# A decode block's tail: wo in one transfer, a layer norm with accumulated sums, and reader-less matmuls moved ahead of wo

## The chip, the cores and the metric

The kernel runs on one core of a Trainium2 chip. The metric is the device time of one execution in microseconds. The kernel before takes 186.57 us (median of 3 runs, 186.53 to 186.63).

## What is computed

One decode step of a block with modulated layer norms, attention over a cache, and a gated FFN, for two tokens (batch 2, one position) of width 640:

```python
mod = (silu(c) @ w_mod).reshape(2, 6, 1, 640)          # sa, ca, ga, sb, cb, gb
h = layernorm(x) * (1 + ca) + sa
q = (h @ wq) as 32 heads of 192
k, v = the last 1024 of 4096 cached positions, 32 heads of 192
o = softmax(q k^T / sqrt(192)) v
x = x + ga * (o @ wo)                                   # wo: 6144 x 640
h = layernorm(x) * (1 + cb) + sb
out = x + gb * ((gelu(h @ w_gate) * (h @ w_up)) @ w_down)   # F = 1536
```

The layer norm has no weights of its own and an epsilon of 1e-5. All inputs are bf16. With two tokens each weight and each cache element is used for next to nothing but two rows: 77 MB are read from HBM.

## The kernel before

**Order and queues.** The kernel is an order written by hand. Each engine has a list of operations (`S.op`, `S.dma`), and the helper derives the semaphore waits from the names of what an operation reads and writes. Each engine works off its list in order. All loads of weights and cache go out from SP's queue, in the order w_mod, wq, four loads of K, four of V, wo, w_gate, w_up, w_down. The few rows of `c` and `x` and the result go through ACT's queue.

**Places.** Three places of 128 partitions x 49,152 bytes hold K and V in turn (two halves of `pp`, and the start of `r1`). wq and later wo (61,440 bytes a partition) lie in `r1`; w_mod and later the three FFN weights lie in `pp`. A load is issued when the last reader of its place is done: wo after the last PV matmul of the first token (`keep["pv", 0, NTL - 1]`), the FFN weights after the second of four PV groups of the second token (`dead`, L595).

**wo.** Partition p holds rows 48p to 48p+47 of wo. `WO_SPLIT = [32, 16]` (L160) cuts them into two transfers, of 40,960 and 20,480 bytes per partition, each with a semaphore and a group of matmuls of its own (L607 to L615): for each row index t four matmuls of 160 columns, one in each quarter of the array, 128 in the first group and 64 in the second, all into one bank. `w_down` is cut likewise, into 8, 3 and 1 of 12 (L162).

**The layer norm** (L350 to L376) is used twice. Its values lie with a token's 640 columns in four groups of partitions, 160 columns each, two tokens side by side. DVE squares `X2[:, 0]` into `X2[:, 1]`, reduces both to two sums per partition (`st2`), a small f32 matmul with `Bsel` adds them over the partitions of a token (L355), and DVE and ACT make mean, variance, root and reciprocal as 128x1 columns. Three DVE instructions over 160 columns follow (`xn`, `mulc`, `out`), and a DVE transpose makes `hT`, the weights of the next matmuls.

**Matmuls without a reader.** `warm(n, bk)` (L455) issues n bf16 matmuls of 384 columns on `ident_b` and `qbc` into a bank that nobody reads. The K phase has four ahead of each reduction; in the tail three stand between gate and up (L634) and five after up (L638).

**The tail**, in TensorE's order: the PV matmuls of the second token, `sel` (four matmuls, L558, which bring the attention result into the layout of wo's weights, `oT`), wo, the statistics of the second layer norm, gate, three `warm`, up, five `warm`, and down in three groups (L648). DVE has `ga_attn` and `x1` (L617, L619) between wo and the layer norm, `geglu` (L639) and a transpose before down, and `gb_y` and `outC` at the end. ACT has the gelu (L635), which writes `gl`, a part of `Sg`, where the scores were.

Of the kernel before, what the change touches and what calls it, by code (L numbers as in the profile page):

```python
# [103 lines left out]
def bass_adaLN_cond__sliding_block_cached__geglu_ffn__decode_kernel(  # L104
# [15 lines left out]
    P = 128  # L120
# [19 lines left out]
    NPR = KP // PJ  # L140
    JH = J // 2
    NH = PJ // JH
# [9 lines left out]
    EPS = 1e-5  # L152
# [4 lines left out]

    NP = 3
    SL = PJ * Dh
    WO_SPLIT = [32, 16]  # L160
    assert sum(WO_SPLIT) == NT and NT * QP == Dh
    WD_SPLIT = [8, 3, 1]  # L162
    assert sum(WD_SPLIT) == FT
# [8 lines left out]
    with es:  # L172
        S = _Sched(nc, es)
        sb = lambda name, shape, dt: es.enter_context(nc.sbuf_tensor(name, shape, dt))
# [22 lines left out]
        ident_f = sb("ident_f", [P, P], F32)  # L197
# [3 lines left out]
        Bsel = sb("Bsel", [P, P], F32)  # L201
# [8 lines left out]
        X2 = sb("X2", [P, 2, DN], F32)  # L210
        st2 = sb("st2", [P, 2], F32)
        mv = sb("mv", [P, 4], F32)
        rstd = sb("rstd", [P, 1], F32)
        modC = sb("modC", [P, 6, DN], F32)
        opc = sb("opc", [P, 2, DN], F32)
        lnt = sb("lnt", [P, 2, DN], F32)
        hC = sb("hC", [P, DN], BF16)
        hT = sb("hT", [P, KT, SQ], BF16)

        Sg = sb("Sg", [P, max(2 * KP, FN)], F32)  # L220
        S_sb = Sg[:, 0:2 * KP].rearrange("p (b r) -> p b r", b=2)
        gl = Sg[:, 0:FN]
# [10 lines left out]
        ps = es.enter_context(nc.psum_tensor("ps", [P, 8, 512], F32))  # L233

        BK_T = 2
# [9 lines left out]
        def bank(k):  # L245
            return ("bank", k)
# [14 lines left out]
        def k_dma(dst, src):  # L261
            return lambda e: e.dma_start(dst, src)  # L262


        def rows_of(tile):
            return tile[0:P:BS, :]

        def dram_rows(v):
            return v.rearrange("b (j n) -> j b n", j=NJ)
# [2 lines left out]
        S.op("pool", lambda e: e.memset(xc[:, :], 0.0), writes=["xc"], name="xc0")  # L272
        S.op("pool", lambda e: e.memset(cx[:, :, :], 0.0), writes=["cxa", "cxb"], name="cx0")
        S.op("pool", lambda e: e.memset(scx[:, :, :], 0.0), writes=["scx"], name="scx0")
        S.dma("act", k_dma(rows_of(cc), dram_rows(c[:, :])), sem_c, writes=["cc"], name="ld_c")
        S.dma("act", k_dma(rows_of(xc), dram_rows(A_x[:, 0, :])), sem_x, writes=["xc"], name="ld_x")
        S.dma("act", k_dma(cx[:, :, 0:XS * KT], c[:, 0:XP * XS * KT].rearrange("b (i n) -> i b n", i=XP)), sem_cx, writes=["cxa"], name="ld_cxa")
# [5 lines left out]
             reads=["Sk"], writes=["ident_f"], name="ident_f")  # L283
        S.op("pool", lambda e: e.tensor_copy(out=ident_b[:, :], in_=ident_f[:, :]),
             reads=["ident_f"], writes=["ident_b"], name="ident_b")
# [33 lines left out]
        for o in range(4):  # L319
# [5 lines left out]
              sem_wq, writes=place_keys(2) + ["wq"], name="ld_wq")  # L325
# [21 lines left out]
        to_contraction(scT[:, :, :], sc[:, :], KT, ["sc"], ["scT"], "scT")  # L347
        S.op("dve", lambda e: e.tensor_copy(out=X2[:, 0, :], in_=xc[:, :]), reads=["xc"], writes=[("X2", 0)], name="x_f32")

        def layer_norm(tag, opc_idx, s_idx):  # L350
            S.op("dve", lambda e: e.tensor_tensor(out=X2[:, 1, :], in0=X2[:, 0, :], in1=X2[:, 0, :], op=ALU.mult),
                 reads=[("X2", 0)], writes=[("X2", 1)], name=tag + "_sq")
            S.op("dve", lambda e: e.tensor_reduce(out=st2[:, :], in_=X2[:, :, :], axis=AX.X, op=ALU.add),
                 reads=[("X2", 0), ("X2", 1)], writes=["st2"], name=tag + "_sum")
            S.op("pe", lambda e: e.matmul(ps[:, BK_T, SC:SC + 2], lhsT=Bsel[:, :], rhs=st2[:, :], start=True, stop=True),  # L355
                 reads=["st2", "Bsel"], writes=[bank(BK_T)], name=tag + "_stat")
            S.op("dve", lambda e: e.tensor_scalar(out=mv[:, 0:2], in0=ps[:, BK_T, SC:SC + 2], scalar1=1.0 / D, scalar2=None, op0=ALU.mult),
                 reads=[bank(BK_T)], writes=[("mv", 0)], name=tag + "_mean")
            S.op("dve", lambda e: e.scalar_tensor_tensor(out=mv[:, 2:3], in0=mv[:, 0:1], scalar=-1.0, in1=mv[:, 0:1],
                                                         op0=ALU.mult, op1=ALU.mult),  # L360
                 reads=[("mv", 0)], writes=[("mv", 1)], name=tag + "_nmsq")
            S.op("dve", lambda e: e.scalar_tensor_tensor(out=mv[:, 2:3], in0=mv[:, 1:2], scalar=EPS, in1=mv[:, 2:3],
                                                         op0=ALU.add, op1=ALU.add),
                 reads=[("mv", 0), ("mv", 1)], writes=[("mv", 1)], name=tag + "_var")
            S.op("act", lambda e: e.activation(out=mv[:, 3:4], in_=mv[:, 2:3], func=ACTF.Sqrt),
                 reads=[("mv", 1)], writes=[("mv", 2)], name=tag + "_sqrt")
            S.op("dve", lambda e: e.reciprocal(out=rstd[:, :], in_=mv[:, 3:4]),
                 reads=[("mv", 2)], writes=["rstd"], name=tag + "_rstd")
            S.op("dve", lambda e: e.tensor_scalar(out=lnt[:, 0, :], in0=X2[:, 0, :], scalar1=mv[:, 0:1], scalar2=rstd[:, 0:1],
                                                  op0=ALU.subtract, op1=ALU.mult),  # L370
                 reads=[("X2", 0), ("mv", 0), "rstd"], writes=[("lnt", 0)], name=tag + "_xn")
            S.op("dve", lambda e: e.tensor_tensor(out=lnt[:, 1, :], in0=lnt[:, 0, :], in1=opc[:, opc_idx, :], op=ALU.mult),
                 reads=[("lnt", 0), ("opc", opc_idx)], writes=[("lnt", 1)], name=tag + "_mulc")
            S.op("dve", lambda e: e.tensor_tensor(out=hC[:, :], in0=lnt[:, 1, :], in1=modC[:, s_idx, :], op=ALU.add),
                 reads=[("lnt", 1), ("modC", s_idx // 3)], writes=["hC"], name=tag + "_out")
            to_contraction(hT[:, :, :], hC[:, :], KT, ["hC"], ["hT"], tag + "_T")  # L376

        MB = (7, 4)
# [76 lines left out]
        def warm(n, bk):  # L455
            def f(e):
                last = None
                for i in range(n):
                    put = e.matmul if i == 0 else lambda *a, **k: held(e, *a, **k)
                    last = put(ps[:, bk, 0:2 * Dh], lhsT=ident_b[:, :], rhs=qbc[:, :, :].rearrange("p b d -> p (b d)"),  # L460
                               start=True, stop=True)
                return last
            S.op("pe", f, reads=["ident_b", "qbc"], writes=[bank(bk)], name="warm")
# [122 lines left out]
        assert state["next"] == len(items)  # L586
        p_sel()

        wo_src = A_wo.rearrange("(p t) n -> p t n", t=NT)
        wo_of = [(sum(WO_SPLIT[:i]), sum(WO_SPLIT[:i + 1])) for i in range(len(WO_SPLIT))]  # L590
        for i, (ta, tb) in enumerate(wo_of):
# [5 lines left out]
              writes=["wg"], deps=dead, name="ld_wg")  # L597
        S.dma("sp", k_dma(wu_v.rearrange("p k n -> p (k n)"), B_w_up.rearrange("(p k) n -> p (k n)", k=KT)), sem_wu,
              writes=["wu"], deps=dead, name="ld_wu")
# [7 lines left out]
        for i, (ta, tb) in enumerate(wo_of):  # L607
            def f(e, ta=ta, tb=tb):
# [7 lines left out]

        S.op("dve", lambda e: e.tensor_tensor(out=lnt[:, 0, :], in0=ps[:, BK_M, 0:DN], in1=modC[:, 2, :], op=ALU.mult),  # L617
             reads=[bank(BK_M), ("modC", 0)], writes=[("lnt", 0)], name="ga_attn")
        S.op("dve", lambda e: e.tensor_tensor(out=X2[:, 0, :], in0=lnt[:, 0, :], in1=X2[:, 0, :], op=ALU.add),  # L619
             reads=[("lnt", 0)], writes=[("X2", 0)], name="x1")  # L620
        layer_norm("ln2", 1, 3)

        def ffn_gu(bk, wv, key, name, ka, kb):
# [7 lines left out]
            S.op("pe", f, reads=["hT", key], writes=[bank(bk)], name="ffn_" + name)  # L631

        ffn_gu(BK_G[0], wg_v, "wg", "wg", 0, KT)
        warm(3, MB[0])  # L634
        S.op("act", lambda e: e.activation(out=gl, in_=ps[:, BK_G[0], 0:FN], func=ACTF.Gelu_apprx_tanh),  # L635
             reads=[bank(BK_G[0])], writes=["gl"], name="gelu")
        ffn_gu(BK_G[1], wu_v, "wu", "wu", 0, KT)
# [56 lines left out]
```

## Time and profile before

| | |
|---|---|
| median of 3 runs | 186.57 us |
| profiled execution, time | 186.42 us |
| profiled execution, span | 185.1 us |
| read from HBM | 76.88 MB, 415 GB/s over the span |
| queue of SP | 2596 packets, 76.87 MB, 96.8% of 16 engines' span |
| TensorE (matmul) busy | 110.3 us, 60% |
| VectorE (DVE) busy | 101.4 us, 55% |
| ScalarE (ACT) busy | 14.7 us, 8% |
| chain that ended last | DMA 56%, DVE 31%, PE 8% |

The span runs from the first to the last instruction; the time of an execution is a little more. Times inside the profile count from the span's start. PE is TensorE, PEld its weight loads, DVE VectorE, ACT ScalarE, POOL GpSimd, and SP the engine that issues the loads. A bracket behind an instruction says how long the engine had sat idle before it, and what ended the wait. The chain is followed back from the last instruction, at each step to what released it.

### The profile page before, as it was taken

Reading aid. Unit: us, or ns where it says so; the run is one execution under the profiler, and the core shown is the slowest. Engines: PE = TensorE matmul, PEld = TensorE weight load, DVE = VectorE, ACT = ScalarE, POOL = GpSimd, SP = SyncE. Lnnn points to the kernel's source line nnn. Section 1 sums busy time; section 2 is a strip of 40 time slices with the busy share of each in tenths; the row PEclk is TensorE's granted clock in tenths of the full one; section 3 lists DMA queues with packets and bytes.
Section 4 is the critical chain, followed back from the end, with each engine's and each line's share of the span. In section 5 each row is a group of like instructions: output and inputs, shape, how many; then the busy total and the mean of one; then the engine's idle time right before and its main releaser. Section 6 shows DMA issues by size and latency. Waiting matters only on the chain.

```text
span 185.1 us, 1892 instructions
## 1 busy us (share of the span) xinstructions
PE 110.3 (60%) x951; PEld 36.7 (20%) x721; DVE 101.4 (55%) x106; ACT 14.7 (8%) x24; POOL 5.3 (3%) x14
## 2 busy tenths in 40 slices
PE   0004900672079999988999885499468059093372
PEld 0001500340000000000000000266256036082211
DVE  5822400010588999999999994747565400302431
ACT  1103410023000000000000000200100000400310
POOL 8300000000000000000000000000000000000000
PEclk9999999998559999999999999569978858858579
DMA  7999999899999989899999989899999999899991
GB/s 261 392 486 469 451 425 417 372 471 404 446 435 414 490 350 510 382 467 396 446 446 404 488 361 499 372 488 396 446 425 425 453 434 425 376 417 427 420 389 58
DMA packets 2699, 76.99 MB, mean 416 GB/s; under 512 B 388, under 2 KB 644, under 8 KB 772
## 3 DMA queue, kind: packets, MB, share of 16 engines
q1 hardware_dynamic: 2596, 76.87, 96.8%
q8 instruction: 6, 0.10, 0.2%
q10 hardware_dynamic: 96, 0.01, 0.0%
q14 instruction: 1, 0.01, 0.0%
HBM read 76.88 MB, written 0.00 MB: 415 GB/s over the span
## 4 chain that ended last, share of the span: by engine, by line
DMA 56%; DVE 31%; PE 8%; SPq 3%; issue 1%; DVEq 0%
DMA pp<-in_A_k_cache_dram 23%; DMA pp<-in_B_w_down_dram 20%; DVE pp L467 19%; DMA pp<-in_A_v_cache_dram 12%; DVE r L467 7%; DVE Sg L487 5%; PE ps L533 4%; PE ps L453 3%; SPq L262 3%; PE ps L480 1%; PE ps L648 0%; DVE lnt L654 0%; DVE sc L656 0%; DVEq L93 0%; SPq L93 0%
## 5 line engine op out<-in xcount | busy, mean ns | idle before, releaser
L467 DVE TENSOR_TENSOR pp<-pp,qbc 128x6144 bf16<-128x6144 bf16 x12 | 40.1, 3348 | 8.5 <-DMA pp<-in_A_k_cache_dram 8.5
L453 PE MATMUL ps<-pp,ident_b 128*128 128x512 bf16 x132 | 31.7, 391 | 0.0
L533 PE MATMUL ps<-pp,Em 128*64 128x384 bf16 x192 | 21.5, 397 | 12.8 <-DMA pp<-in_A_v_cache_dram 11.6
L518 DVE TENSOR_TENSOR Em<-E_sb,M32b 128x2048 bf16<-128x2048 bf16 x8 | 18.2, 2288 | 7.2 <-PE ps L533 6.5
L533 PEld LDWEIGHTS ps<-pp,Em 128*64 128x64 bf16 x192 | 14.5, 134 | 19.5 <-issue 7.8
L467 DVE TENSOR_TENSOR r<-r,qbc 128x6144 bf16<-128x6144 bf16 x4 | 13.4, 3345 | 0.0
L389 PE MATMUL ps<-pp,scT 128*32 128x480 bf16 (+1 forms) x40 | 4.4, 595 | 14.7 <-DMA pp<-in_w_mod_dram 14.7
L487 DVE TENSOR_REDUCE Sg<-ps 128x32 f32<-128x512 f32 x16 | 10.9, 682 | 3.3 <-PE ps L453 3.3
L480 PE MATMUL ps<-pp,ident_b 128*128 128x512 bf16 x12 | 4.9, 407 | 12.7 <-DVE pp L467 12.7
L453 PE MATMUL ps<-qbc,ident_b 128*128 128x384 bf16 x54 | 12.1, 333 | 0.0
L423 PE MATMUL ps<-r,hT 128*32 128x512 bf16 x60 | 5.3, 532 | 10.6 <-DMA r<-in_A_wq_dram 10.6
L453 PE MATMUL ps<-r,ident_b 128*128 128x512 bf16 x44 | 10.1, 379 | 0.0
L550 DVE TENSOR_SCALAR On<-ps,rden 32x192 bf16<-32x192 f32 x4 | 1.7, 418 | 15.1 <-PE ps L533 15.1
L460 PEld LDWEIGHTS ps<-qbc,ident_b 128*128 128x128 bf16 x18 | 1.8, 98 | 37.8 <-issue 37.8
L434 DVE CAST qC<-ps 128x512 bf16<-128x512 f32 x1 | 0.7, 691 | 15.1 <-PE ps L423 15.1
L612 PE MATMUL ps<-r,oT 128*32 128x160 bf16 x192 | 5.8, 303 | 5.2 <-DMA r<-in_A_wo_dram 5.2
L507 ACT ACTIVATE E_sb<-Sg,nb 128x256 bf16<-128x256 f32 x2 | 1.0, 500 | 72.4 <-DVE nb L505 72.4
L460 PE MATMUL ps<-qbc,ident_b 128*128 128x384 bf16 x18 | 6.0, 336 | 0.7 <-ACT qbc L432 0.7
L612 PEld LDWEIGHTS ps<-r,oT 128*32 128x32 bf16 x192 | 5.3, 129 | 5.7 <-DMA r<-in_A_wo_dram 5.7
L617 DVE TENSOR_TENSOR lnt<-ps,modC 128x160 f32<-128x160 f32 x1 | 0.3, 324 | 10.4 <-PE ps L612 10.4
L480 PEld LDWEIGHTS ps<-pp,ident_b 128*128 128x128 bf16 x12 | 1.2, 97 | 23.3 <-DVE pp L467 22.7
L533 PE MATMUL ps<-r,Em 128*64 128x384 bf16 x64 | 5.4, 327 | 0.0
(82 smaller groups left out, 67.6 us busy)
## 6 DMA issues: line engine op xcount, KB each, us to landing
pp<-in_A_k_cache_dram SPq DMA_DIRECT2D x3, 6144.0 KB, 39.5
pp<-in_A_v_cache_dram SPq DMA_DIRECT2D x3, 6144.0 KB, 23.7
r<-in_A_wq_dram SPq DMA_DIRECT2D x1, 7680.0 KB, 28.9
r<-in_A_k_cache_dram SPq DMA_DIRECT2D x1, 6144.0 KB, 38.0
r<-in_A_v_cache_dram SPq DMA_DIRECT2D x1, 6144.0 KB, 23.4
r<-in_A_wo_dram SPq DMA_DIRECT2D x1, 5120.0 KB, 30.6
pp<-in_w_mod_dram SPq DMA_DIRECT2D x1, 4720.0 KB, 13.8
r<-in_A_wo_dram SPq DMA_DIRECT2D x1, 2560.0 KB, 36.3
```

The source lines that it names most:

```text
L262: return lambda e: e.dma_start(dst, src)
L389: last = e.matmul(ps[SQ * j:SQ * j + SQ, bk, 0:ni * DN].rearrange("p (i n) -> p i n", i=ni), lhsT=scT[:, k, :], rhs=pp_f[:, o:o + 3 * D].r ...
L423: last = e.matmul(ps[SQ * j:SQ * j + SQ, BK_H + c, 0:QW], lhsT=hT[:, k, :], rhs=wq_v[:, k, RN * j + QW * c:RN * j + QW * (c + 1)], start=( ...
L453: return e.add_instruction(i)
L460: last = put(ps[:, bk, 0:2 * Dh], lhsT=ident_b[:, :], rhs=qbc[:, :, :].rearrange("p b d -> p (b d)"), start=True, stop=True)
L467: S.op("dve", lambda e: e.tensor_tensor(out=places[k][:, JH * q:JH * (q + 1), :], in0=places[k][:, JH * q:JH * (q + 1), :], in1=qbc[:, b, ...
L480: last = put(o_ap, lhsT=ident_b[:, :], rhs=places[k][:, JH * q:JH * (q + 1), ci * GC:(ci + 1) * GC], start=(ci == 0), stop=(ci == NCH - 1))
L487: S.op("dve", lambda e: e.tensor_reduce(out=S_sb[:, b, a:a + JH], in_=ps[:, q % 2, 0:JH * GC].rearrange("p (j c) -> p j c", j=JH), axis=AX ...
L518: S.op("dve", lambda e: e.tensor_tensor(out=Em[:, t % 2, :, :], in0=E_sb[:, b, J * t:J * (t + 1)].unsqueeze(2).broadcast_to([P, J, H]), in ...
L533: last = e.matmul(ps[r:r + 2 * H, BK_O[b], 0:ON], lhsT=Em[:, t % 2, 2 * jp:2 * jp + 2, :].rearrange("p j c -> p (j c)"), rhs=places[k][:, ...
L550: S.op("dve", (lambda rows, cols: lambda e: e.tensor_scalar(out=On[rows, b, :], in0=ps[rows, BK_O[b], cols], scalar1=rden[rows, b:b + 1], ...
L612: last = e.matmul(ps[SQ * j:SQ * j + SQ, BK_M, 0:DN], lhsT=oT[:, t, :], rhs=wo_v[:, t, DN * j:DN * j + DN], start=(t == 0), stop=(t == NT ...
```

## The change

wo comes in one transfer, and its 192 matmuls form one group behind one semaphore. The layer norm takes its sums from accumulator outputs: the sum of squares from the squaring itself, the sum of x from the instruction that makes it (`x1`) or, for the first layer norm, from a reduction ahead of it (`x_sum`). The variance is made negated in one instruction, and the root takes the sign and the epsilon as its scale and bias (`epsc`, a new constant written by POOL). The product with 1 + c comes before that with the reciprocal root, in two DVE instructions instead of three, the first of which (`xmc`) does not need the root. The three `warm` between gate and up go; ten f32 matmuls of 480 columns on `ident_f` and `Sg` (`warm_f`) come into TensorE's list between `sel` and wo, into bank 7, which nobody reads.

```diff
-    WO_SPLIT = [32, 16]
+    WO_SPLIT = [48]
...
+        epsc = sb("epsc", [P, 1], F32)
...
+        S.op("pool", lambda e: e.memset(epsc[:, :], EPS), writes=["epsc"], name="epsc")
...
+        S.op("dve", lambda e: e.tensor_reduce(out=st2[:, 0:1], in_=X2[:, 0, :], axis=AX.X, op=ALU.add),
+             reads=[("X2", 0)], writes=[("st2", 0)], name="x_sum")
+
         def layer_norm(tag, opc_idx, s_idx):
-            S.op("dve", lambda e: e.tensor_tensor(out=X2[:, 1, :], in0=X2[:, 0, :], in1=X2[:, 0, :], op=ALU.mult),
...
-            S.op("dve", lambda e: e.tensor_reduce(out=st2[:, :], in_=X2[:, :, :], axis=AX.X, op=ALU.add),
...
+            S.op("dve", lambda e: e.scalar_tensor_tensor(out=X2[:, 1, :], in0=X2[:, 0, :], scalar=1.0, in1=X2[:, 0, :],
+                                                         op0=ALU.mult, op1=ALU.mult, accum_out=st2[:, 1:2]),
...
-            S.op("dve", lambda e: e.scalar_tensor_tensor(out=mv[:, 2:3], in0=mv[:, 0:1], scalar=-1.0, in1=mv[:, 0:1],
-                                                         op0=ALU.mult, op1=ALU.mult),
...
-            S.op("dve", lambda e: e.scalar_tensor_tensor(out=mv[:, 2:3], in0=mv[:, 1:2], scalar=EPS, in1=mv[:, 2:3],
-                                                         op0=ALU.add, op1=ALU.add),
...
-            S.op("act", lambda e: e.activation(out=mv[:, 3:4], in_=mv[:, 2:3], func=ACTF.Sqrt),
...
+            S.op("dve", lambda e: e.scalar_tensor_tensor(out=mv[:, 2:3], in0=mv[:, 0:1], scalar=mv[:, 0:1], in1=mv[:, 1:2],
+                                                         op0=ALU.mult, op1=ALU.subtract),
...
+            S.op("act", lambda e: e.activation(out=mv[:, 3:4], in_=mv[:, 2:3], func=ACTF.Sqrt, scale=-1.0, bias=epsc[:, :]),
...
+            S.op("dve", lambda e: e.scalar_tensor_tensor(out=lnt[:, 1, :], in0=X2[:, 0, :], scalar=mv[:, 0:1], in1=opc[:, opc_idx, :],
+                                                         op0=ALU.subtract, op1=ALU.mult),
...
             S.op("dve", lambda e: e.reciprocal(out=rstd[:, :], in_=mv[:, 3:4]),
...
-            S.op("dve", lambda e: e.tensor_scalar(out=lnt[:, 0, :], in0=X2[:, 0, :], scalar1=mv[:, 0:1], scalar2=rstd[:, 0:1],
-                                                  op0=ALU.subtract, op1=ALU.mult),
...
-            S.op("dve", lambda e: e.tensor_tensor(out=lnt[:, 1, :], in0=lnt[:, 0, :], in1=opc[:, opc_idx, :], op=ALU.mult),
...
-            S.op("dve", lambda e: e.tensor_tensor(out=hC[:, :], in0=lnt[:, 1, :], in1=modC[:, s_idx, :], op=ALU.add),
...
+            S.op("dve", lambda e: e.scalar_tensor_tensor(out=hC[:, :], in0=lnt[:, 1, :], scalar=rstd[:, 0:1], in1=modC[:, s_idx, :],
+                                                         op0=ALU.mult, op1=ALU.add),
...
+        def warm_f(n, bk):
+            def f(e):
+                last = None
+                for i in range(n):
+                    last = e.matmul(ps[:, bk, 0:480], lhsT=ident_f[:, :], rhs=Sg[:, 0:480], start=True, stop=True)
+                return last
+            S.op("pe", f, reads=["ident_f", "gl"] + [("S", b, t, q) for b in range(2) for t in range(NPR) for q in range(NH)],
+                 writes=[bank(bk)], name="warm_f")
+
+        warm_f(10, MB[0])
+
...
-        S.op("dve", lambda e: e.tensor_tensor(out=X2[:, 0, :], in0=lnt[:, 0, :], in1=X2[:, 0, :], op=ALU.add),
-             reads=[("lnt", 0)], writes=[("X2", 0)], name="x1")
+        S.op("dve", lambda e: e.scalar_tensor_tensor(out=X2[:, 0, :], in0=lnt[:, 0, :], scalar=1.0, in1=X2[:, 0, :],
+                                                     op0=ALU.mult, op1=ALU.add, accum_out=st2[:, 0:1]),
+             reads=[("lnt", 0)], writes=[("X2", 0), ("st2", 0)], name="x1")
         layer_norm("ln2", 1, 3)
...
         ffn_gu(BK_G[0], wg_v, "wg", "wg", 0, KT)
-        warm(3, MB[0])
```

More of the change, by code (lines that the diff above doesn't have):

```diff
@@ L348, in bass_adaLN_cond__sliding_block_cached__geglu_ffn__decode_kernel @@
         S.op("dve", lambda e: e.tensor_copy(out=X2[:, 0, :], in_=xc[:, :]), reads=["xc"], writes=[("X2", 0)], name="x_f32")
+        S.op("dve", lambda e: e.tensor_reduce(out=st2[:, 0:1], in_=X2[:, 0, :], axis=AX.X, op=ALU.add),
+             reads=[("X2", 0)], writes=[("st2", 0)], name="x_sum")
         def layer_norm(tag, opc_idx, s_idx):
-            S.op("dve", lambda e: e.tensor_tensor(out=X2[:, 1, :], in0=X2[:, 0, :], in1=X2[:, 0, :], op=ALU.mult),
-                 reads=[("X2", 0)], writes=[("X2", 1)], name=tag + "_sq")
@@ L353, in layer_norm @@
-            S.op("dve", lambda e: e.tensor_reduce(out=st2[:, :], in_=X2[:, :, :], axis=AX.X, op=ALU.add),
-                 reads=[("X2", 0), ("X2", 1)], writes=["st2"], name=tag + "_sum")
+            S.op("dve", lambda e: e.scalar_tensor_tensor(out=X2[:, 1, :], in0=X2[:, 0, :], scalar=1.0, in1=X2[:, 0, :],
+                                                         op0=ALU.mult, op1=ALU.mult, accum_out=st2[:, 1:2]),
+                 reads=[("X2", 0)], writes=[("X2", 1), ("st2", 1)], name=tag + "_sq")
@@ L355, in layer_norm @@
             S.op("pe", lambda e: e.matmul(ps[:, BK_T, SC:SC + 2], lhsT=Bsel[:, :], rhs=st2[:, :], start=True, stop=True),
-                 reads=["st2", "Bsel"], writes=[bank(BK_T)], name=tag + "_stat")
+                 reads=[("st2", 0), ("st2", 1), "Bsel"], writes=[bank(BK_T)], name=tag + "_stat")
             S.op("dve", lambda e: e.tensor_scalar(out=mv[:, 0:2], in0=ps[:, BK_T, SC:SC + 2], scalar1=1.0 / D, scalar2=None, op0=ALU.mult),
                  reads=[bank(BK_T)], writes=[("mv", 0)], name=tag + "_mean")
-            S.op("dve", lambda e: e.scalar_tensor_tensor(out=mv[:, 2:3], in0=mv[:, 0:1], scalar=-1.0, in1=mv[:, 0:1],
-                                                         op0=ALU.mult, op1=ALU.mult),
-                 reads=[("mv", 0)], writes=[("mv", 1)], name=tag + "_nmsq")
@@ L362, in layer_norm @@
-            S.op("dve", lambda e: e.scalar_tensor_tensor(out=mv[:, 2:3], in0=mv[:, 1:2], scalar=EPS, in1=mv[:, 2:3],
-                                                         op0=ALU.add, op1=ALU.add),
-                 reads=[("mv", 0), ("mv", 1)], writes=[("mv", 1)], name=tag + "_var")
-            S.op("act", lambda e: e.activation(out=mv[:, 3:4], in_=mv[:, 2:3], func=ACTF.Sqrt),
-                 reads=[("mv", 1)], writes=[("mv", 2)], name=tag + "_sqrt")
+            S.op("dve", lambda e: e.scalar_tensor_tensor(out=mv[:, 2:3], in0=mv[:, 0:1], scalar=mv[:, 0:1], in1=mv[:, 1:2],
+                                                         op0=ALU.mult, op1=ALU.subtract),
+                 reads=[("mv", 0)], writes=[("mv", 1)], name=tag + "_nvar")
@@ new lines, in layer_norm @@
+            S.op("act", lambda e: e.activation(out=mv[:, 3:4], in_=mv[:, 2:3], func=ACTF.Sqrt, scale=-1.0, bias=epsc[:, :]),
+                 reads=[("mv", 1), "epsc"], writes=[("mv", 2)], name=tag + "_sqrt")
+            S.op("dve", lambda e: e.scalar_tensor_tensor(out=lnt[:, 1, :], in0=X2[:, 0, :], scalar=mv[:, 0:1], in1=opc[:, opc_idx, :],
+                                                         op0=ALU.subtract, op1=ALU.mult),
+                 reads=[("X2", 0), ("mv", 0), ("opc", opc_idx)], writes=[("lnt", 1)], name=tag + "_xmc")
@@ L367, in layer_norm @@
             S.op("dve", lambda e: e.reciprocal(out=rstd[:, :], in_=mv[:, 3:4]),
                  reads=[("mv", 2)], writes=["rstd"], name=tag + "_rstd")
-            S.op("dve", lambda e: e.tensor_scalar(out=lnt[:, 0, :], in0=X2[:, 0, :], scalar1=mv[:, 0:1], scalar2=rstd[:, 0:1],
-                                                  op0=ALU.subtract, op1=ALU.mult),
-                 reads=[("X2", 0), ("mv", 0), "rstd"], writes=[("lnt", 0)], name=tag + "_xn")
-            S.op("dve", lambda e: e.tensor_tensor(out=lnt[:, 1, :], in0=lnt[:, 0, :], in1=opc[:, opc_idx, :], op=ALU.mult),
-                 reads=[("lnt", 0), ("opc", opc_idx)], writes=[("lnt", 1)], name=tag + "_mulc")
@@ L374, in layer_norm @@
-            S.op("dve", lambda e: e.tensor_tensor(out=hC[:, :], in0=lnt[:, 1, :], in1=modC[:, s_idx, :], op=ALU.add),
-                 reads=[("lnt", 1), ("modC", s_idx // 3)], writes=["hC"], name=tag + "_out")
+            S.op("dve", lambda e: e.scalar_tensor_tensor(out=hC[:, :], in0=lnt[:, 1, :], scalar=rstd[:, 0:1], in1=modC[:, s_idx, :],
+                                                         op0=ALU.mult, op1=ALU.add),
+                 reads=[("lnt", 1), "rstd", ("modC", s_idx // 3)], writes=["hC"], name=tag + "_out")
```

## The prediction

> **What bounds the kernel now.** I read the chain of waits first. From 113 us on it is almost only transfers: the load of V, one burst of PV matmuls that frees a place for the FFN weights, and then one long piece until the last piece of w_down has landed. Only 0.7 us of matmuls and two DVE instructions follow it.
>
> ```profile
> 113.25 22.49 DMA pp<-in_A_v_cache_dram
> 135.75 0.14 issue
> 135.88 7.09 PE ps L533 x64
> ...
> 144.31 37.67 DMA pp<-in_B_w_down_dram
> 181.98 0.04 issue
> 182.02 0.39 PE ps L648 x12
> 182.41 0.01 issue
> 182.42 0.28 PE ps L648 x4
> ```
>
> Second, TensorE's rows in the timeline (start, length, line, what the idle time before it waited for). The matmuls of wo start on a landing (162.44 and 168.55), gate (first L628) starts on hT, which the layer norm makes, and up (second L628) and both starts of down (L648) on landings again. So every matmul of the tail but gate waits for bytes, and gate has slack: it ends at 176.53, while w_up lands at 177.7.
>
> ```profile
> 162.44 4.46 PE L612 MATMUL ps<-r,oT 128*32 128x160 bf16 x128 [3.60 <-DMA r<-in_A_wo_dram]
> 168.55 1.36 PE L612 MATMUL ps<-r,oT 128*32 128x160 bf16 x64 [1.65 <-DMA r<-in_A_wo_dram]
> 171.57 0.59 PE L355 MATMUL ps<-st,Bsel 128*128 128x2 f32 x2 [1.66 <-DVE st L353]
> 174.74 1.79 PE L628 MATMUL ps<-pp,hT 128*32 128x384 bf16 x20 [2.58 <-DVE hT L344]
> ...
> 177.74 1.00 PE L628 MATMUL ps<-pp,hT 128*32 128x384 bf16 x20
> ...
> 180.94 0.74 PE L648 MATMUL ps<-pp,aT 128*32 128x160 bf16 x32 [1.29 <-DMA pp<-in_B_w_down_dram]
> 182.02 0.66 PE L648 MATMUL ps<-pp,aT 128*32 128x160 bf16 x16 [0.34 <-DMA pp<-in_B_w_down_dram]
> ```
>
> Third, the same stretch by windows (length, busy time of the engines, granted clock, DMA share, GB/s). The DMA engines are full to 179.8, then some finish before others (0.74, 0.39).
>
> ```profile
> 159.00:162.40 3.40, 0.00 (x0) 0.00 (x0) 0.51 (x1) 0.68 (x1) 0.00 (x0) 0.75 0.80 343
> 162.40:166.90 4.50, 4.46 (x128) 4.14 (x128) 0.00 (x0) 0.00 (x0) 0.00 (x0) 0.50 0.97 415
> 166.90:168.50 1.60, 0.00 (x1) 0.00 (x0) 0.00 (x0) 0.00 (x0) 0.00 (x0) 0.81 1.05 433
> 168.50:170.00 1.50, 1.36 (x64) 1.13 (x64) 0.04 (x1) 0.00 (x0) 0.00 (x0) 1.00 1.01 430
> 170.00:173.00 3.00, 0.59 (x2) 0.50 (x2) 1.89 (x7) 0.20 (x1) 0.00 (x0) 0.66 1.00 425
> 174.70:177.70 3.00, 2.86 (x23) 0.71 (x21) 0.00 (x0) 0.49 (x1) 0.00 (x0) 0.50 0.99 413
> 177.70:178.70 1.00, 0.96 (x21) 0.48 (x21) 0.00 (x0) 0.00 (x0) 0.00 (x0) 0.97 0.92 375
> 179.80:180.90 1.10, 0.00 (x0) 0.00 (x0) 0.50 (x1) 0.00 (x0) 0.00 (x0) 1.00 0.74 296
> 180.90:182.00 1.10, 0.74 (x32) 0.56 (x32) 0.00 (x0) 0.00 (x0) 0.00 (x0) 1.00 0.39 146
> ```
>
> The clock column is either 1.00 or 0.50, so a value between dates the switch: 0.75 puts a fall at 160.7, 0.81 a rise at 167.5, 0.66 a fall at 170.96, 0.97 a rise at 177.76. These lie 6.8, 3.4 and 6.8 us apart, a grid of 3.4 us. Per grid stretch: it fell after one with 1.36 us of matmuls (167.5 to 171, 40% busy), rose after one 82% busy (164.1 to 167.5), stayed full through one 62% busy (177.8 to 181.2), and stayed at half through one 48% busy (160.7 to 164.1).
>
> **The change part by part.** The sum is made against the profiled execution: span 185.10 us, time 186.42; the median of the runs is 186.57, 0.15 above it.
>
> *One transfer for wo.* The pair lands at 162.42 and 168.53. V landed before it at 150.40, so 5.24 MB took 12.02 us and 2.62 MB took 6.11 us: with 8 rows per DMA engine, 1.503 us for 40,960 bytes and 0.764 us for 20,480. Two of the short make 1.528, so one more packet costs 0.025 us, and 8 per engine 0.20 us. The FFN weights (15,360-byte rows, gate and up in 9.19 us, 0.574 us a row) make it 0.011 us, so 0.09. Against it stands wq, which already has 61,440-byte rows: 19.19 us from the landing of w_mod to its own, 1.06 us above wo's 18.13, though with small pieces of w_mod between. So the price is -0.20 to +1.06; I take -0.10, since the wo and FFN rows are nearest and wq's window shares its time. Everything queued behind wo (gate, up, three of down) shifts with it, and so does the end. SP issues one transfer less at 131.78; its next issue waits for PV until 142.99, so that half of 0.81 us hides in 10 us of waiting.
>
> *wo's matmuls in one group.* All 192 now start at 168.5, and no 128 of them run before it. The 64 warm ones took 1.36 us with a single one at 0.23, so 0.018 each: 192 take 3.65 us at the full clock (end 172.2 instead of 169.91). The 128 at half clock give 0.0325 each, 6.5 us at worst.
>
> *The ten f32 matmuls.* Nobody reads their bank, but they stand ahead of wo in TensorE's queue, from 158.87 on (the sel matmuls end at 158.85; what they read, the scores, was finished at 113.9). The trace has no f32 matmul of 480 columns. Each f32 call is two instructions (L355, x2). Lower bound: bf16 speed, 384 columns per 0.163 us in the warm group at 42.75, so 480 in 0.20 and a call in 0.41 us. Upper: the lone f32 transpose at L495, 128 columns in 0.271 us with nothing overlapped, so 1.02 per instruction and 2.03 per call. I take 0.82: bf16 instructions of 96 and 192 columns last 0.204 and 0.246 us, so 128 would last 0.218; the f32 one's 0.053 more is the streaming time of 128 columns once again, hence half speed, 0.41 an instruction. Ten end at 167.1, 1.4 us before the landing: cost nothing, hidden by the landing of wo. Every grid stretch from 157.3 to 171 is then at least 69% busy, so wo runs at the full clock.
>
> *The layer norm.* From wo's end to gate it took 4.83 us (169.91 to 174.74). Gone: the reduce (0.49 + 0.04), one 128x1 instruction (0.20), the wait for ACT (0.27, now under xmc), xn and mulc (0.39 + 0.36); new on the path: xmc (0.36) and the reciprocal as before. That leaves 3.5 us. Two accumulator outputs come on top: between nothing and 0.20 each (ACT's accum_out at L507 shows as an extra instruction of 0.186). I take the middle, 3.7. Gate starts at 172.2 + 3.7 = 175.9, 1.2 us later than now. The first layer norm and x_sum lie before 34 us, where wq lands 12 us after hT is ready: nothing. The memset of epsc delays POOL by 0.2 us and with it DVE's table building, which is finished at 10.3 against w_mod's landing at 14.7: nothing.
>
> *No matmuls between gate and up.* They filled the stretch to 177.76 and lifted the clock for up. Now the stretch to 174.35 holds some 1.4 us of wo and 0.6 of the statistics, 43 to 60% busy, where the rows show a fall (40%) and no fall (62%). I take half clock for both: gate 1.79 us to 177.7, up, also 1.79, to 179.5, 0.8 us later than the 178.74 of now. [...]
>
> *Where it is absorbed.* From the end of up to the first possible down matmul is 1.6 us (178.74 to 180.34: geglu, transpose). The first 32 of down take 0.74 and must be over when the second piece lands at 182.0, so up may end at 179.68. At 179.5 it does. Sum: -0.1 for the packets, 0 for all else, rounded up by 0.05 for a tight down group: 186.57 - 0.05 = 186.5 us. Its own range, 186.2 to 186.9, is the 0.2% (0.37 us) that a measurement here can tell from no change.
>
> **The rivals.**
> *Too long a filler (slower, my rival of the other side), 0.11.* If f32 weights (0.25 us each at L355) load serially, a call takes 0.82 + 0.50 = 1.32 and ten end at 172.1; wo ends at 175.7, gate starts at 179.4, up ends at 181.4, the 48 of down (48 x 0.018 + 0.23 = 1.1) run from 183.0 to 184.1 instead of 182.70: 187.9 us. It decides from about 1.0 us a call (up at half clock) or 1.14 (full). [...] Against it: the 16 pairs at L443 take 1.49 us, 0.093 each, where 0.082 of streaming and 0.079 of loading would make 0.161 serially; that is bf16, and no f32 stream exists here.
> *Too short a filler, 0.06.* At 0.41 a call the ten end at 163.0, the clock falls at 167.5, wo takes up to 6.5 us and some 1.5 us reach the end: 188.0.
> *Cold from gate to down, 0.06.* Another phase of the grid keeps down at half clock too: 48 of them 1.6 us instead of 1.1, from 181.2; 187.1.
> *The long rows are no better than wq's, 0.07.* +1.06 on the landing of everything behind: 187.6.
> *Transfers gain more than a packet's price, 0.20.* The last 2.2 us show engines ending unevenly; were they even, 0.26 x 1.1 + 0.61 x 1.1 = 0.95 us would go, 185.6; half of it 186.1. For it: one completion less per engine. Against it: w_down's last piece landed 0.40 us after the one before, its 0.16 MB alone being 0.38 at 432 GB/s, so a boundary costs next to nothing.
>
> **How the numbers follow.** No change 0.50; slower 0.11 + 0.06 + 0.06 + 0.07 = 0.30; faster 0.20. The range 185.9 to 187.7 holds the forecast, half the uneven gain and the rivals up to the long rows; outside stay the full uneven gain (below, 0.05) and the two wrong fillers (above, 0.13 together, as they reach past 187.7).
>
> **What would show it.** Ten f32 calls of about 0.82 us ending near 167; all of wo from one landing at 168.4 in some 3.7 us; the chain still ending in w_down's load; up ending before 179.7. I am wrong if down starts on aT rather than on a landing, if TensorE reaches wo after 170, or if w_down's last landing moves by more than 0.3 us.

## The result

The changed kernel takes 189.46 us (median of 5 runs, 188.92 to 189.79) against 186.57 us: a ratio of 1.0148, 95% interval 1.0135 to 1.016, so 2.9 us or 1.5% slower. The prediction was 186.5 us, no change, with a range of 185.9 to 187.7. The profiled execution took 189.46 us, with a span of 188.2.

The chain of waits of the changed kernel (start, length, what) no longer runs through the load of w_down. It goes through the landing of wo, and then through a piece that nothing in the program accounts for:

```profile
131.78 36.64 DMA r<-in_A_wo_dram
168.42 0.04 issue
168.46 2.95 PE ps L623 x160
171.41 3.44 issue
174.85 1.28 PE ps L623 x25
176.13 0.02 issue
```

TensorE does 160 of wo's 192 matmuls, stands still for 3.44 us, and does the other 32. All 192 are one operation behind one semaphore, so no wait of the program lies between them; the profile files the gap under "issue", time in which the engine waited for nothing that it shows. TensorE's rows of the changed kernel in the timeline:

```profile
158.66 8.28 PE L593 MATMUL ps<-Sg,ident_f 128*128 128x480 f32 x20
...
168.46 2.95 PE L623 MATMUL ps<-r,oT 128*32 128x160 bf16 x160 [1.52 <-DMA r<-in_A_wo_dram]
174.85 1.26 PE L623 MATMUL ps<-r,oT 128*32 128x160 bf16 x32 [3.44 <-issue]
...
179.70 3.39 PE L640 MATMUL ps<-pp,hT 128*32 128x384 bf16 x40 [1.84 <-DVE hT L346]
...
184.71 0.81 PEld L659 LDWEIGHTS ps<-pp,aT 128*32 128x32 bf16 x48 [1.59 <-DVE aT L346]
184.71 1.01 PE L659 MATMUL ps<-pp,aT 128*32 128x160 bf16 x48
```

Gate and up run as one stretch of 40, without a wait for w_up between them, and down starts on aT and not on a landing. The whole tail now hangs on TensorE, DVE and ACT. The transfers finish when they did before (a DMA share of 0.36 from 180.9 to 182.0, against 0.39), as the windows of the changed kernel show (columns as in the prediction):

```profile
171.40:173.00 1.60, 0.01 (x4) 0.00 (x0) 0.00 (x0) 0.00 (x0) 0.00 (x0) 1.00 0.96 404
173.00:174.85 1.85, 0.00 (x0) 0.00 (x0) 0.00 (x0) 0.00 (x0) 0.00 (x0) 0.85 1.03 432
174.85:176.20 1.35, 1.26 (x32) 0.93 (x31) 0.04 (x1) 0.00 (x0) 0.00 (x0) 0.50 0.97 413
...
180.90:182.00 1.10, 1.10 (x20) 0.56 (x16) 0.00 (x0) 0.46 (x1) 0.00 (x0) 0.50 0.36 134
```

No compute engine works during the stop, and the DMA engines are full. The clock falls within it (0.85 in the second window), so the last 32 matmuls run at half clock.

### The profile page after: what moved, and what is told of

The parts are those of the page before. It is cut to its first block, busy times and chain, and to the rows that moved or that the text cites. A ratio compares the mean times of both kernels' runs of the same rounds, so it can differ in the third digit from the quotient of the medians.

```text
span 188.2 us, 1926 instructions
## 1 busy us (share of the span) xinstructions
PE 116.6 (62%) x968; PEld 39.2 (21%) x740; DVE 99.9 (53%) x104; ACT 14.9 (8%) x24; POOL 5.3 (3%) x15
## 4 chain that ended last, share of the span: by engine, by line
DMA 42%; DVE 35%; PE 17%; issue 3%; SPq 2%; ACT 0%; DVEq 0%
DMA pp<-in_A_k_cache_dram 23%; DMA r<-in_A_wo_dram 19%; DVE pp L467 19%; DVE r L467 7%; PE ps L533 7%; DVE Sg L487 5%; PE ps L453 4%; SPq L263 2%; PE ps L623 2%; PE ps L640 2%; DVE Em L518 1%; PE ps L659 1%; PE ps L480 1%; DVE M L493 0%; ACT E_sb L507 0%
## 5 line engine op out<-in xcount | busy, mean ns | idle before, releaser
L453 PE MATMUL ps<-qbc,ident_b 128*128 128x384 bf16 x52 | 11.8, 340 | 0.0
L593 PE MATMUL ps<-Sg,ident_f 128*128 128x480 f32 x20 | 8.3, 570 | 0.0
L623 PE MATMUL ps<-r,oT 128*32 128x160 bf16 x192 | 4.2, 250 | 5.0 <-issue 3.4
L460 PE MATMUL ps<-qbc,ident_b 128*128 128x384 bf16 x17 | 5.7, 336 | 0.7 <-ACT qbc L432 0.7
```

What stands on the lines that cost most here:

```text
L453: return e.add_instruction(i)
L593: last = e.matmul(ps[:, bk, 0:480], lhsT=ident_f[:, :], rhs=Sg[:, 0:480], start=True, stop=True)
L623: last = e.matmul(ps[SQ * j:SQ * j + SQ, BK_M, 0:DN], lhsT=oT[:, t, :], rhs=wo_v[:, t, DN * j:DN * j + DN], start=(t == 0), stop=(t == NT ...
```

## The theories

Theory F: the stop is the wait for TensorE's own next instructions. The page of the profile counts 6 packets and 0.10 MB on a queue of kind "instruction", about 0.017 MB each, and in the window of the stop one of them takes 6.1% of the 16 DMA engines beside 90.2% for the data. The theory supposes that these packets bring TensorE's list in blocks, the next one while the current one runs; the profile names neither the block nor the request. The page has 968 matmuls and 740 weight loads, 1,708 in all, so some 285 to a packet if all 6 are TensorE's. The theory takes 256 for a block, and the runs below try that number: with 256 instructions added the stop is back at its place, with 64 or 128 it is gone. wo issues a weight load and a matmul every 0.0184 us (2.95 / 160), so 256 instructions, 128 such pairs, last 2.36 us here. If the load of the next block takes longer, TensorE would starve at the border, the place in its list where one block ends and the next begins. By the theory, where that is depends on the count of instructions alone.

Theory W: something in wo's data or place. Theory P: TensorE pauses after dense work, whatever its instructions. Both keep the stop at the same matmul when instructions are added elsewhere.

## The experiments

### Instructions added far ahead of the tail

Four runs add 64, 128, 32 and 256 instructions (one weight load, then tiny matmuls without loads, into bank 7, nobody reads them) in the gap ahead of q (the product with wq), where TensorE idles. The run with 256 has 128 of them there and 128 ahead of the first matmuls of w_mod. Nothing in the tail is touched.

```diff
         mod_part(1)
         load_next()
+        dead_pe(64, MB[0])
```

> In the changed kernel TensorE stops for 3.44 us in the middle of wo, after 160 of 192 matmuls (171.41 to 174.85), and the profile names no semaphore for it. Here 64 matmul instructions without a reader (one weight load, 63 tiny matmuls) stand ahead of q, where TensorE idles for 10 us; the tail is untouched. Theory F (the stop is the wait for the next block of TensorE's instructions, whose load has to pass the loaded DMA engines): the stop moves 64 instructions, that is 32 pairs of weight load and matmul, earlier, to after matmul 128 of wo. The matmul before it is reached 0.6 us earlier, so the stop is shorter or equal, 0 to 3.5 us, depending on when the load was asked for; total 186.5 to 189.5. Theory W (something of wo's data or place): the stop stays after matmul 160, 3.4 us, 189.4 us. Theory P (TensorE pauses after so much dense work): it stays as well, since the work ahead of wo in the tail is the same.

> As the run before with 128 instructions ahead of q. Theory F with blocks of 256 instructions: block borders fall after matmul 96 of wo, where the block before was entered at the end of the PV matmuls, 10 us earlier, and 64 instructions behind wo's end, in gate; both loads have time, the stop goes, wo runs from 168.4 to about 172.0 in one piece, gate starts at 175.6, and the total is 186.3 to 186.8 us. If the block or the lead is of another size, the stop sits after matmul 96 and is still there. Theories W and P: a stop of 3.4 us after matmul 160, 189.4 us.

> 32 more TensorE instructions ahead of q. Theory F: the border moves from after matmul 160 of wo to after matmul 144, and the block before it is entered at matmul 16 instead of 32, 0.3 us after wo begins: a stop of 3.0 to 3.5 us after matmul 144, 189 to 189.5 us. A theory in which the stop belongs to a fixed point of wo has it after 160 or not at all.

> With 64 and 128 more TensorE instructions ahead of the tail the stop in wo was gone and the time that of the kernel before (186.52 and 186.51 us). Here 256 more (128 ahead of the first matmuls of w_mod, 128 ahead of q). Theory F with blocks of 256 instructions: the borders lie where they lay in the changed kernel, the stop is back after matmul 160 of wo, 3 to 3.5 us, 189 to 189.5 us. If instead it is any displacement that helps (the work ahead of q, another start of the kernel's phases), there is no stop and 186.5 us.

| instructions added | wo's matmuls before the stop | stop, us | instruction packet, us | wo goes on at, us | time, us | ratio to before (95%) |
|---|---|---|---|---|---|---|
| 0 (changed kernel) | 160 | 3.44 | 172.3 to 173.3 | 174.85 | 189.46 | 1.0148 (1.0135 to 1.016) |
| 32 | 145 | 3.17 | 172.0 to 173.1 | 174.40 | 188.81 | 1.0123 (1.0103 to 1.0144) |
| 64 | no stop | 0 | 164.0 to 165.1 | | 186.52 | 1.0001 (0.9991 to 1.0012) |
| 128 | no stop | 0 | 159.6 to 160.7 | | 186.51 | 0.9994 (0.9984 to 1.0004) |
| 256 | 161 | 2.93 | 172.3 to 173.3 | 174.65 | 188.84 | 1.0125 (1.0105 to 1.0146) |

The packets come from the DMA view, cut to narrow windows. For the changed kernel from 172 to 173 us it has one packet on the instruction queue; 6.1% of 16 engines over 1 us is one engine for 0.98 us:

```profile
q1 hardware_dynamic: 32, 0.38, 90.2%
q8 instruction: 1, 0.02, 6.1%
```

The timeline rows of wo, first of the run with 32 added, then of the one with 256, then of the one with 64:

```profile
168.50 2.73 PE L635 MATMUL ps<-r,oT 128*32 128x160 bf16 x145 [1.20 <-DMA r<-in_A_wo_dram]
174.40 1.26 PE L635 MATMUL ps<-r,oT 128*32 128x160 bf16 x47 [3.17 <-issue]
```

```profile
168.71 3.01 PE L636 MATMUL ps<-r,oT 128*32 128x160 bf16 x161 [0.35 <-DMA r<-in_A_wo_dram]
174.65 0.73 PE L636 MATMUL ps<-r,oT 128*32 128x160 bf16 x31 [2.93 <-issue]
```

```profile
168.47 3.50 PE L635 MATMUL ps<-r,oT 128*32 128x160 bf16 x192 [1.09 <-DMA r<-in_A_wo_dram]
...
175.36 1.79 PE L652 MATMUL ps<-pp,hT 128*32 128x384 bf16 x20 [1.84 <-DVE hT L346]
177.72 1.79 PE L652 MATMUL ps<-pp,hT 128*32 128x384 bf16 x20 [0.56 <-DMA pp<-in_B_w_up_dram]
```

Instructions issued some 145 us earlier move the stop. 32 instructions move it by 15 pairs of load and matmul (16 expected), 256 bring it back to within one matmul of its place, and 64 or 128 remove it. With 64 the border should fall after matmul 128. The block ahead of that border then begins at wo's first matmul or before, and the next block's packet has ended at 165.1, while TensorE is still at the f32 matmuls ahead of wo. With 128 the border should fall after matmul 96, and the packet has ended at 160.7. In the three runs with a stop the packet falls into the stop, and the matmuls go on 1.3 to 1.6 us after its end. Theories W and P fall, and theory F fits all five kernels. The period of 256 instructions is what the runs show together: with 256 added the stop is back, and with 128 added, where any shorter period that divides 256 would have kept it, it is gone. In three of the five kernels the load is not hidden: they stop for 2.93 to 3.44 us.

### No data traffic while wo runs

The FFN loads wait for wo's last matmul instead of the PV group.

```diff
-        dead = [keep["pv", 1, NTL // 2 - 1]]
+        dead = [keep["wo"]]
```

> The changed kernel with the loads of the three FFN weights issued only when the last matmul of wo is done, so that the DMA engines have nothing to move while wo runs; the instructions of TensorE are the same in number and order. It is slower as a whole by design: 5.9 MB (13.8 us at 427 GB/s) after wo's end at about 172 instead of beside it, some 190 to 193 us. Theory F with the load held up by other traffic: the stop after matmul 160 shrinks to under 1 us or goes. Theory F with a load of fixed length whatever the traffic: a stop of 3.4 us. Theories W and P: a stop of 3.4 us.

Measured: 195.01 us, 2 us over what was expected (w_gate lands 7.6 us after its issue). The stop is still after 160 matmuls, but shorter. Here is the chain of waits of this run, and its DMA view from 168.6 to 172, with the instruction packet as the only one:

```profile
168.51 2.95 PE ps L610 x160
171.46 0.50 issue
171.96 0.76 PE ps L610 x32
```

```profile
DMA packets 1, 0.02 MB, mean 5 GB/s; under 512 B 0, under 2 KB 0, under 8 KB 0
q8 instruction: 1, 0.02, 1.7%
```

Suppose that the load is asked for when the block before is entered, 256 instructions or 128 matmuls ahead of the border. Then its length is the end of the stop less the time of that matmul. Here: matmul 32 at 168.51 + 32 x 0.0184 = 169.1, to 171.96, 2.9 us. In the changed kernel: 169.05 to 174.85, 5.8 us. So with the traffic the load took twice as long here, 5.8 us against 2.9. The packet shows where: without traffic it runs from 169.6 to 170.5, 0.5 us after the entry, and in the changed kernel from 172.3, 3.2 us after it. The packet itself (0.9 and 1.0 us) and the time from its end to the next matmul (1.4 and 1.6 us) are nearly the same. Both variants of theory F had a part of it right: 2.9 us are there without traffic, and about as much again is spent ahead of the packet with it.

### The data in shorter rows

w_gate and w_up in five transfers each, of 3,072-byte rows.

```diff
-        S.dma("sp", k_dma(wg_v..., B_w_gate...), sem_wg, writes=["wg"], deps=dead, name="ld_wg")
...
+            for k in range(KT):
+                S.dma("sp", k_dma(wv[:, k, :], src.rearrange("(p k) n -> p k n", k=KT)[:, k, :]), sems[k],
+                      writes=[(key, k)], deps=dead, name="ld_%s%d" % (key, k))
```

> The changed kernel with w_gate and w_up in five transfers each, of 3,072-byte rows instead of 15,360, so that the packets that stand beside the load of the instruction block from 168.5 to 175 are a fifth as long; all else, the count of TensorE's instructions but for some waits behind wo included, as in the changed kernel. With no data traffic at all the stop was 0.50 us instead of 3.44. Theory R (the block's packets take turns with packets of the data, one for one): the load gets shorter, the stop shrinks to under 1.5 us, total 186.5 to 187.5. Theory B (it waits for bytes already queued or outstanding, whatever their packets): the stop stays at 3 to 3.5 us; total 189 to 189.8.

Measured: 189.76 us, ratio 1.0169 (1.0152 to 1.0186). The stop is 3.20 us, after 160 matmuls; from matmul 32 at 169.2 to 174.76 the load took 5.6 us, with its packet from 172.3 to 173.4. Data packets a fifth as long do not shorten the wait ahead of it (3.1 us from the entry to the packet's start, 3.2 in the changed kernel), so nothing here shows it taking turns with the data packet by packet. What it waits for in the DMA engines stays open.

### One transfer for wo, by itself

```diff
-    WO_SPLIT = [32, 16]
+    WO_SPLIT = [48]
```

> The kernel before with wo in one transfer and one group of matmuls, nothing else of the change. The count of instructions ahead of wo is 40 less than in the changed kernel (ten f32 calls of two loads and two matmuls), so the border is after matmul 180 or so and the block before is entered at 52. Without the f32 matmuls wo begins at half clock (0.0325 us a matmul): 52 at 170.2, 180 at 174.3. Theory F with a load of 5.8 us from that entry: ready at 176.0, a stop of about 1.7 us, wo ends at 176.3, the old layer norm of 4.83 us brings gate to 181.1 and the total to about 189.5 to 190.5. Were there no stop: wo ends at 174.8, gate starts at 179.7, total 188.5 to 189. So one transfer costs 2 us or more by itself, through wo's late start.

Measured: 191.52 us, ratio 1.0268 (1.0248 to 1.0288), slower than the whole change and 1 us over what was expected. The timeline of this run:

```profile
168.66 6.06 PE L612 MATMUL ps<-r,oT 128*32 128x160 bf16 x180 [9.67 <-DMA r<-in_A_wo_dram]
175.73 0.39 PE L612 MATMUL ps<-r,oT 128*32 128x160 bf16 x12 [1.01 <-issue]
```

The border is after matmul 180, as counted from the 40 instructions of the f32 matmuls that are not there. At 6.06 / 180 = 0.0337 us each, matmul 52 comes at 170.4, and 175.73 - 170.4 = 5.3 us is the load (packet from 173.1 to 174.2). From the entry to the border TensorE takes 4.3 us here and 2.4 in the changed kernel. The stop is shorter by somewhat more than these 1.9 us (1.01 against 3.44), and the load is 5.3 us against 5.8. That supports the count from the entry of the block before.

### The changed kernel with wo in two transfers

```diff
-    WO_SPLIT = [48]
+    WO_SPLIT = [32, 16]
```

> The changed kernel with wo in two transfers again (32 and 16 rows, two groups of matmuls); the ten f32 matmuls, the new layer norm and the empty place between gate and up stay. Theory F: the count of instructions is the same (but for one wait), so the block border is still near matmul 160 of wo, but the first 128 run from 162.4 on, the border of the block before is passed at 167 instead of 169, and the last 64 start on the landing at 168.5: the load has 2 us more and most of the stop goes; wo ends at 170 to 172, total 186.3 to 187.0. But the ten f32 matmuls end at 166.9, so the first 128 cannot start at 162.4 and run from 166.9 to 169.3. Theory W: no stop. Theory that the loss is in the other parts (f32 matmuls, empty place): 189.4 us.

Measured: 187.65 us, executions from 186.47 to 188.81, ratio 1.0055 (1.0025 to 1.0085). The ten f32 matmuls hold the first group until 166.44, and when the second group's turn comes its data have landed:

```profile
166.44 2.95 PE L623 MATMUL ps<-r,oT 128*32 128x160 bf16 x160
172.50 0.74 PE L623 MATMUL ps<-r,oT 128*32 128x160 bf16 x32 [3.11 <-issue]
```

The groups run into one another at the same pace, and the stop is there with 3.11 us (packet from 170.2 to 171.3). I had expected it to be mostly gone: I had let the second group wait for a landing at 168.5, and it did not wait. The stop lies 2 us earlier, and in this execution, of 186.58 us, it is absorbed. Why others of the same kernel took up to 2.2 us more no trace here shows.

### The layer norm by itself, and the f32 matmuls taken away

The first is the kernel before with the new layer norm alone. The second is the changed kernel without `warm_f`, with 160 instructions added far ahead so that no border disturbs wo.

> The kernel before with the new layer norm alone (accumulator outputs, two instructions fewer over the columns, epsc); wo in two transfers, no f32 matmuls, three matmuls between gate and up as before. The layer norm took 3.4 to 3.6 us from wo's end to gate in the changed kernel's variants, against 4.83. Gate would start at 173.4 instead of 174.7, but up still waits for w_up until 177.7 and down for w_down until 181 and 182: my theory (the end is set by the transfers, and the layer norm has slack) gives no change, 186.3 to 186.8 us. If the layer norm were on the path: 185.2 us.

> The changed kernel without the ten f32 matmuls, and with 160 tiny TensorE instructions far ahead of the tail, which put the block border at matmul 100 of wo or so, its block entered before wo, and the next border behind wo's end. What is left to see is the price of the clock: no stop in wo, but half clock from 168.5 (0.0325 us a matmul, 6.1 us), wo's end at 174.6, the short layer norm of 3.5 us, gate and up at half clock in 3.4 us from 178.1, down at 183.1: 188.0 to 188.8 us. If the f32 matmuls bring nothing: 186.5 us.

The layer norm alone: 186.50 us, ratio 0.9997 (0.9987 to 1.0006). No change, as expected: in its profile up and both starts of down wait for their landings. Without the f32 matmuls: 187.65 us, ratio 1.0057 (1.0036 to 1.0079), a little under what was expected: wo's 192 took 5.67 us, 0.0295 each, between the 0.0348 of the kernel before at a clock of 0.50 (4.46 / 128) and the 0.0182 of an undisturbed wo at 1.00 (3.50 / 192), so I take it that the clock rose while wo ran. The chain of this run:

```profile
168.53 0.04 issue
168.57 5.70 PE ps L635 x157
174.27 0.02 issue
...
177.64 3.39 PE ps L652 x21
```

Against the 3.50 us of wo with the f32 matmuls and no stop, 2.2 us are lost and 1.1 of them reach the end. So the f32 matmuls are worth 1.1 us here, and together with one transfer and an undisturbed wo they come out even with the kernel before.

### The uneven end of the transfers

```diff
-        for o in range(4):
-            S.dma("sp", k_dma(wx_v[o:XP:4, 0:XS, :], wx_src[o:XP:4]), sem_wx[0], writes=[("wx", o)], name="ld_wx%d" % o)
+        S.dma("sp", k_dma(wx_v[0:XP, 0:XS, :], wx_src), sem_wx[0], writes=[("wx", o) for o in range(4)], name="ld_wx")
```

> The kernel before with the small rows of w_mod (120 rows of 640 bytes) in one transfer of 12 partitions instead of four of 3, nothing else. It tries the premise of the rival that transfers could gain: the DMA engines end unevenly (share 0.74 and 0.39 in the last 2.2 us), which would be worth 0.95 us were they even. If the uneven end comes from these small rows lying on three engines: the last landing moves from 182.0 to 181.2 or so and the total to 185.6 to 186.1. If it comes from elsewhere, 186.5 us.

Measured: 187.61 us, ratio 1.0053 (1.0035 to 1.007), 0.5% slower. w_mod's first matmuls start at 15.67 instead of 14.69, and the tail is 1.0 to 1.4 us later (down's last matmuls start at 183.26 instead of 182.02). The DMA engines still end unevenly, with shares of 0.95, 0.56 and 0.26 in the three windows from 179.8 to 183.0. Nothing bears out my reason for the uneven end, and what makes it stays open. No version that beats both kernels came out of the runs.

## Why the prediction was wrong, point by point

**The step that failed** is "wo's matmuls in one group": "192 take 3.65 us at the full clock (end 172.2 instead of 169.91)". The rate was right: undisturbed they take 3.50 us. The unbroken stream was not; from 168.46 to 176.13 they took 7.67 us, of which 3.44 are the stop and 0.7 the half clock after it. I took a rate from 64 matmuls and stretched it over 384 instructions, more than one block, without asking where the instructions come from. No rival held this, and the range ended 1.8 us short. One of the prediction's own signs came true: "I am wrong if down starts on aT rather than on a landing".

**How 4.1 us became 2.9.** Against the run with 64 instructions added, wo ends 4.1 us later (176.13 and 172.0), up ends 3.6 us later (183.09 and 179.51), since without the stop it had waited 0.56 us for w_up, and down ends 3.1 us later (185.74 and 182.65); the medians differ by 2.94. The second half microsecond is no slack but the clock: down takes 1.01 us at full clock after the stop, and 1.47 us without it, where the clock was 0.50 from 180.9 to 182.0.

**One transfer:** forecast -0.10 us on the landings. From the first PV matmul of the last group to wo's first matmul it is 18.13 us before (150.42 to 168.55) and 18.06 after (150.40 to 168.46), so -0.07: right. The rival of the long rows is out. So is the one in which transfers gain, since their end did not move. The prediction's price of a packet from the FFN rows is a little low: four rows of 0.574 us are 2.297, against 2.266 for the pair of wo's rows, two packets more, so 0.016 us a packet and not 0.011. That is 0.13 us for 8, within the range that it gave.

**The f32 matmuls:** forecast 0.41 us an instruction, the ten ending at 167.1, hidden. Measured 20 instructions in 8.28 us, ending at 166.94. Right, and both rivals of a wrong filler are out. One of them had the f32 weight loads run serially. The loads here lie inside the matmuls: each load takes 0.19 us, and each matmul still starts 0.40 us after the last, so nothing was added, and the trace decides against it for this stream.

**The layer norm:** forecast 3.7 us from wo's end to gate. Measured 3.57 (176.13 to 179.70), 3.36 where wo was undisturbed. An accumulator output cost next to nothing here:

```profile
176.51 0.32 DVE L630 SCALAR_TENSOR_TENSOR X<-lnt,X 128x160 f32<-128x160 f32 x1
176.77 0.08 DVE L630 DVE_READ_ACCUMULATOR X<-lnt,X 128x1 f32 x1
176.88 0.32 DVE L356 SCALAR_TENSOR_TENSOR X<-X 128x160 f32<-128x160 f32 x1
```

These rows of the changed kernel show the extra instruction with 0.08 us, begun before the first one's end; the next starts 0.37 after the first, as without it (0.36).

**Gate and up at half clock, and where it is absorbed:** without the stop both did run at half clock. With 64 added, up ends at 179.51 (forecast 179.5), and the total is 186.52 (forecast 186.5). That it is so close is partly luck. The layer norm was done sooner than forecast, gate ended at 177.15 and not at 177.7, and up then waited for w_up until 177.72. The end is also reached by another path than the forecast's, as the chain of that run shows:

```profile
141.66 36.01 DMA pp<-in_B_w_up_dram
177.67 0.04 issue
177.72 1.79 PE ps L652 x20
179.51 0.43 PE ps L472
179.94 1.28 PE ps L465 x4
181.22 1.42 PE ps L671 x44
```

Down follows up and the matmuls without a reader, and does not wait for w_down. It starts on aT, so the prediction's sign of being wrong holds without the stop too. It ends at 182.65, where it ended at 182.70 in the kernel before: there it had waited 0.34 us for the last piece of w_down, here it ran in part at half clock. With 128 added gate ran at full clock (1.02 us), up at half (1.79), and down at half as well (1.79, to 183.02), at a median of 186.51 (the profiled execution took 186.77). So a cold down, the rival of 0.06, occurred and cost next to nothing; its own figures, 181.2 + 1.6 = 182.8 against 182.70, give 186.7 and not 187.1. The forecast is the time of the change without the stop, but not in every step its path.

**Why the kernel before has no stop.** By the count its border is at matmul 180 too, as in the run with one transfer, but its first group starts at 162.44, so matmul 52 comes at 162.44 + 52 x 0.0348 = 164.2, and a load of 5.3 us is there at 169.5, when 180 is reached (168.55 + 51 x 0.018 + 0.03). The trace has the packet from 167.0 to 168.0, during the wait for wo's second piece. The stops ended 1.2 to 1.6 us after their packet, which would be 169.2 to 169.6 here. The split of wo gave the load its time, by a margin of almost nothing. The margin is worked out, not shown: no run moved this border.

## What to carry to other kernels

A long stretch of small instructions, here 384 at one every 9 to 17 ns, outran the supply of the instructions themselves: it stopped for 0.50 us beside idle DMA engines and for 1.01 to 3.44 us beside full ones. Where a stretch is longer than the period of 256 found here, check where the borders fall, and give the block ahead of a border time: the loads took up to 5.8 us at the stops here. A stop inside one operation, filed under "issue", was the sign. The DMA view tells whether a packet of the instruction queue falls into it, and some dead instructions far ahead tell whether it moves. Merging transfers also merges the matmuls behind them into one dense stretch, so price the stretch and not only the transfer.

## What was not expected of the hardware

- The place of TensorE's stop has a period of 256 instructions: 256 more bring it back to after matmul 161, where it had been after 160, and 64 or 128 more remove it. Taken as the load of a block, and counted from the entry of the block before, it took 5.3 to 5.8 us in the runs with full DMA engines and 2.9 us in the one with idle ones. The packet started 2.7 to 3.2 us after that entry, against 0.5 us. It took 0.9 to 1.1 us in all of them, and the matmuls went on 1.2 to 1.6 us after its end. That the load is asked for at the entry is inferred, since the profile times the packet and not the request. It rests on the like lengths over borders after 145, 160, 161 and 180 matmuls and at two paces. It does not fit every border with one and the same wait: the next packet of the changed kernel starts at 180.2, 5.3 us after the border at 174.85.
- 120 rows of 640 bytes in one transfer of 12 partitions made the first large landing 1.0 us later than in four transfers of 3 (15.67 against 14.69 us). Why stays open.
